# Opening of a linear-attention and expert kernel: other load order, buffers per head pair, and seven PSUM banks for the first products

## The chip, the cores and the metric

The kernel runs on one core of a Trainium2 chip. The metric is the device time of one execution in microseconds (us), median of several executions. Where the time of a profiled execution is meant I say "span": it is some 2 us shorter than the device time. All comparisons use executions in the fast state unless I say otherwise (an execution more than 1.5% above the fastest of the same kernel counts as slow). I call a kernel faster or slower where the 95% interval of the ratio excludes 1. The granted clock is the share of TensorE's full clock that the profile records as granted; 1.00 is full speed. Ratios are the mean time of one kernel's fast runs over that of the other's of the same rounds, so they are not quite the ratio of the medians that I quote.

## The reference, cut to what matters

```python
# q, k, v: (8 batches, 8 heads, 576 rows, 64), fp32
phi = lambda x: where(x > 0, x, exp(x) - 1) + 1
kv  = einsum('bhsd,bhse->bhde', phi(k), v)        # per head: 64 x 64
z   = phi(k).sum(rows)
x   = (phi(q) @ kv) / (phi(q) @ z + 1e-6)         # -> (4608, 512)
p   = domain_probs / domain_probs.sum(-1)
for e in range(4):                                # dense experts
    out += p[:, e] * (relu(x @ w1[e]) @ w2[e])    # 512 -> 1024 -> 512
```

The heads are worked on in four pairs of two (128 partitions each). The experts need x turned (x^T), because the kernel hands the matmuls their operands with the contracted index on the partitions.

## The kernel before: the parts that matter here

Every operation is handed to a planner with a priority, an estimated duration, and keys that it reads and writes. The planner simulates the engines and emits the instructions in the order that this gives. The framework then adds a wait wherever two engines touch the same tile.

The opening handles the first 512 rows of batch 0: four head pairs of attention, whose turned x feeds the first layer (`L681`, later `L761` and near it) and the second layer (`L691`, later `L772`) of the four experts in turn, while the weights arrive. From about 80 us on, the other rows follow in "units" (`L835`, later `L924`). They use the same weights and are bound by TensorE.

PSUM is the memory that TensorE's products are written to. The kernel takes eight tiles of it, of 128 partitions by 512 fp32. I call each of them a bank:

```python
    l1b = [pp.tile([P, 512], FP32, tag=f"l1b{i}", name=f"l1b{i}") for i in range(3)]
    l2b = [pp.tile([P, 512], FP32, tag=f"l2b{i}", name=f"l2b{i}") for i in range(4)]
    at = pp.tile([P, 512], FP32, tag="at", name="at")
    slot = [at[:, i * 2 * DE : (i + 1) * 2 * DE] for i in range(3)]
    tbank = l2b[3].bitcast(FP16)
```

A pair of the opening goes through them so (cut from `attention`, `two=True`, and `turn_x`):

```python
            tq, tk = (l2b[1].bitcast(FP16), "l2b1") if two else (tbank, "l2b3")   # q turned
            # ...
            kvs_, kvk = l2b[2][:, 0 : 2 * DE], ("l2b2k",)                # phi(k)^T v
            # ...
            den = l2b[2][:, 256 : 256 + 2 * C].rearrange("p (c h) -> p c h", h=2)
            # ... numerators go to `at`
            # turn_x: four transposes into tbank (l2b[3]), then a ScalarE copy to xt0
```

The first layer of expert 0 has eight column groups (`fj`) of four products each (`dc`, one for each pair's x^T). A product of 512 columns takes 0.216 us. Four groups have a bank of their own and can take the products of pairs 0 to 2 before pair 3 is ready. The other four run after it:

```python
        banks = [(l1b[i], "l1b%d" % i) for i in range(3)]
        if nb == 4:
            banks += [(l2b[0], "l2b0")]
        # ...
            for dc in range(DC):
                for fj in range(nb):
                    bank, key = banks[(b0 + fj) % nb]
                    p_ = pri + (dc * 4 + fj) * step
                    pl.add("PE", 0.216, p_,
                           lambda fj=fj, bank=bank, dc=dc: mm1(e, fj, bank, (dc,)),
                           r=w1k(e, dc, fj) + (("s4", 1, dc),), w=(key,))
```

In gaps of the opening `keep_warm` issues filler matmuls (`L1075`, later `L1174`), which only keep the array busy.

Of the kernel before, what the change touches and what calls it, by code (L numbers as in the profile page):

```python
# [20 lines left out]
class Plan:  # L21
# [13 lines left out]
    def __init__(self):  # L35
        self.ops = []
        self.wr = {}
        self.rd = {}

    def add(self, eng, dur, pri, fn, r=(), w=(), move=0.0, after=0.0, lead=1.2):  # L40
        n = len(self.ops)
        deps = set()
        for key in r:
            if key in self.wr:
                deps.add(self.wr[key])
            self.rd.setdefault(key, []).append(n)
        for key in w:
            if key in self.wr:
                deps.add(self.wr[key])
            deps.update(x for x in self.rd.get(key, ()) if x != n)  # L50
        for key in w:
            self.wr[key] = n
            self.rd[key] = []
        self.ops.append(
            dict(eng=eng, dur=dur, pri=pri, fn=fn, deps=deps, move=move, after=after, lead=lead, w=w)
        )
        return n

    def deadlines(self):
# [10 lines left out]
        for n, o in enumerate(ops):  # L70
            if o["eng"] != "PE" and o["pri"] >= -99:
# [62 lines left out]
def kernel(  # L134
# [27 lines left out]
    WARM, COLD = 22.0, 28  # L162
    T0, TU = 79.0, 6.4
# [7 lines left out]
    def sb(name, shape, dt):  # L171
# [47 lines left out]
    v00 = vss[1].rearrange("p h c d -> p (h c d)").bitcast(FP16)[:, 2 * C * D :].rearrange(  # L219
        "p (h c d) -> p h c d", h=2, c=C  # L220
    )
    ones = sb("ones", [P, 2, 1], FP16)
    rc4 = sb("rc4", [P, 2 * C], FP32)
# [20 lines left out]
    def lk(i):  # L244

        return ("l2b2k", "l2b2n") if i == 2 else ("l2b%d" % i,)

    def stage_keys(i):

        if i < 2:  # L250
            return ("st", i, 0), ("st", i, 1), ("st", i, 2)
        return ("xp", 0), ("xp", 1), ("u2", 0)
# [35 lines left out]
    def v16(i):  # L288

        flat = vss[i].rearrange("p h c d -> p (h c d)").bitcast(FP16)  # L290
        return flat[:, 0 : 2 * C * D].rearrange("p (h c d) -> p h c d", h=2, c=C)

    def load_pair(b, pr, queue, pri, after=0.0, hold=None):
        hs = slice(2 * pr, 2 * pr + 2)
        n = 3 if b < 2 else 2
        i = rot("stage%d" % n, n) if n == 2 else rot("stage3", 3)
        stage[b, pr] = i
        kk = stage_keys(i)
        vo = vss[i] if b or queue == "SP" else v16(i)
        parts = [(k, kqs[i][:, 0], kk[0]), (v, vo, kk[2]), (q, kqs[i][:, 1], kk[1])]  # L300
        if b == 0:
            parts[1:] = parts[:0:-1]
        for t, o, key in parts:
            if (b, pr, key) == (0, 0, kk[1]):
                load_rest(0, "SP", 0, parts=(0,))
            keys = (key, "v00") if (b, key) == (1, ("st", 1, 2)) else (key,)
            dma(queue, pri, o, t[b, hs, 0:NT].rearrange("h (p c) d -> p h c d", c=C), keys,
                0.7,
                hold="w" if b == 2 else hold if key == kk[0] else None,
                mark="k0" if (b, pr, key) == (0, 0, kk[0]) else None, after=after)  # L310

    def load_rest(b, queue, pri, after=0.0, parts=(0, 1, 2)):
        par = b % 2
        rs = slice(par * R, par * R + R)
        for i in parts:
            t, o = ((k, kqr[rs, 0]), (v, vr[rs]), (q, kqr[rs, 1]))[i]
            dma(queue, pri, o, t[b, :, NT:S].rearrange("h s d -> s h d"), (("str", par, i),),
                1.1,
                hold="w" if b in (2, 3) else None, after=after)
# [26 lines left out]
    def probs(b0, b1, raw, keys, out_key, pri):  # L346
# [7 lines left out]
            r=keys, w=(out_key,))  # L354
# [10 lines left out]
    def rest_maps(b, pe_mode, pri, parts=(0, 1)):  # L365
# [19 lines left out]
        if not pe_mode:  # L385
            pl.add("SP", 1.25, pri + 1, lambda: nc.sync.dma_start_transpose(
                out=qTr[par][:, :, rs], in_=kqpr[rs, 1].rearrange("p h d -> p (h d)")),
                r=("qpr",), w=[("qTr", par, i) for i in range(DC)], move=0.9, lead=0.2)

# [44 lines left out]
    def attention(b, pr, pe_mode, pri, step, two=False):  # L434
# [16 lines left out]
        zi = pr if two else rot("kvz", 2)  # L451
# [8 lines left out]
        if two:  # L460
            vh = v00 if pr == 0 else v16(si)
            vk = "v00" if pr == 0 else sk[2]

        def vcast():
            if two:
                nc.scalar.copy(vh, vs)
            else:
                nc.scalar.copy(vp[:, :, :, 0:D].rearrange("p c h d -> p h c d"), vs)

        order_ = (0, 1)  # L470
        for i in order_:
# [4 lines left out]
            if i == 0 and not (two and pr):  # L476
                pl.add("ACT", 0.52, pri + step, vcast, r=(sk[2],), w=(vk,))
        if pe_mode:

            tq, tk = (l2b[1].bitcast(FP16), "l2b1") if two else (tbank, "l2b3")  # L480

            def turn():
# [4 lines left out]
                if two:  # L487
                    return
# [7 lines left out]
                   r=(("kqp", pi, 1), "ident") + (() if two else ("qpr",)), w=(tk,))  # L496
            pl.add("ACT", 0.5, pri + 3.5 * step, lambda: nc.scalar.copy(  # L497
                qT.rearrange("p c t -> p (c t)"), tq[:, 0:NT]), r=(tk,), w=(("qT", ti),))
            if not two:
                pl.add("DVE", 0.2, pri + 3.5 * step, lambda: nc.vector.tensor_copy(  # L500
                    qTr[par][:, pr, rs], tq[:, NT : NT + R]), r=(tk,), w=(("qTr", par, pr),))
# [6 lines left out]
        if two:  # L508
            kvs_, kvk = l2b[2][:, 0 : 2 * DE], ("l2b2k",)
        kv3 = kvs_.rearrange("p (h e) -> p h e", h=2)  # L510

        def kv():
            for c in range(C):
                if two:
                    nc.tensor.matmul(out=kv3[:, :, 0:D], lhsT=kp[:, c], rhs=vh[:, :, c],
                                     start=(c == 0), stop=False, skip_group_check=True)
                    nc.tensor.matmul(out=kv3[:, :, D:DE], lhsT=kp[:, c], rhs=ones,
                                     start=False, stop=False, skip_group_check=True)
                else:
                    nc.tensor.matmul(  # L520
                        out=kvs_, lhsT=kp[:, c], rhs=vp[:, c], start=(c == 0), stop=False
                    )
# [6 lines left out]
                skip_group_check=two,  # L529
# [7 lines left out]
        pl.add("PE", 0.42 if two else 0.3, pri + 4 * step, kv,  # L537
# [4 lines left out]

        if two:
            den = l2b[2][:, 256 : 256 + 2 * C].rearrange("p (c h) -> p c h", h=2)

            def nd0():
                for c in range(C):
                    nc.tensor.matmul(out=at[:, c * P : (c + 1) * P], lhsT=qT[:, c],
                                     rhs=kvz[:, :, 0:D], start=True, stop=True)
                    nc.tensor.matmul(out=den[:, c], lhsT=qT[:, c],  # L550
                                     rhs=kvz[:, :, D:DE], start=True, stop=True)

            def norm0():
                rc = rc4.rearrange("p (c h) -> p c h", h=2)
                nc.vector.reciprocal(rc, den)
                nc.vector.tensor_tensor(
                    out=xs[:, :, fs].rearrange("p c (h d) -> p c h d", h=2),
                    in0=at.rearrange("p (c h d) -> p c h d", c=C, h=2),
                    in1=rc[:, :, :, None].broadcast_to([P, C, 2, D]),
                    op=AO.mult,  # L560
                )

            pl.add("PE", 0.36, pri + 5 * step, nd0, r=(("qT", ti), ("kvz", zi)),
                   w=("at", "l2b2n"))
            pl.add("DVE", 0.83, pri + 5.5 * step, norm0, r=("at", "l2b2n"),
                   w=[("x", par, pr, c) for c in range(C)])
            return
# [77 lines left out]
    def sums_w2(e, pri):  # L645
# [11 lines left out]
        for o, a, b_, r, w in (  # L657
# [5 lines left out]
            pl.add("DVE", 0.62, pri, two(o, a, b_), r=r, w=w)  # L663


    def turn_x(pr, pri):
        fs = slice(pr * P, (pr + 1) * P)

        def go():
            for c in range(C):  # L670
                nc.tensor.transpose(
                    out=tbank[:, c * P : (c + 1) * P], in_=x_b[0][:, c, fs], identity=identh
                )

        pl.add("PE", 0.25, pri, go, r=[("x", 0, pr, c) for c in range(C)] + ["ident"], w=("l2b3",))
        pl.add("ACT", 0.5, pri + 0.5, lambda: nc.scalar.copy(xt0[:, pr, :], tbank[:, 0:NT]),
               r=("l2b3",), w=(("s4", 1, pr),))

    def mm1(e, fj, bank, dcs):
        for dc in dcs:  # L680
            nc.tensor.matmul(  # L681
                out=bank,
                lhsT=w1_sb[e][:, dc, fj * P : (fj + 1) * P],
                rhs=xt0[:, dc, :],
                start=(dc == 0),
                stop=(dc == DC - 1),
# [18 lines left out]
    def first_l1(e, pri, step, nb):  # L705
        ht = []
        banks = [(l1b[i], "l1b%d" % i) for i in range(3)]
        if nb == 4:
            banks += [(l2b[0], "l2b0")]
        ht = [rot("ht", len(hts)) for _ in range(FC)]  # L710

        def relu(fj, bank, key, pr_):
            pl.add("ACT", 0.5, pr_, lambda: nc.scalar.activation(hts[ht[fj]], bank, AF.Relu),
# [3 lines left out]
        if nb:  # L717
            b0 = cnt.get("l1", 0) if nb < 4 else 0
            for dc in range(DC):
                for fj in range(nb):  # L720
                    bank, key = banks[(b0 + fj) % nb]
                    p_ = pri + (dc * 4 + fj) * step
                    pl.add("PE", 0.216, p_,
                           lambda fj=fj, bank=bank, dc=dc: mm1(e, fj, bank, (dc,)),
                           r=w1k(e, dc, fj) + (("s4", 1, dc),), w=(key,))
                    if dc == DC - 1:
                        relu(fj, bank, key, p_ + 0.2)
            done = nb
            if nb == 4:
# [282 lines left out]
    load_pair(0, 0, "SP", 0)  # L1012
    load_rest(0, "SP", 0, parts=(1,))
    load_pair(0, 1, "POOL", 0, hold="k0")
    load_pair(0, 2, "POOL", 0)
    rest_maps(0, True, 3, (0,))
    for pr in range(DC):
        if pr == 3:
            load_pair(0, 3, "POOL", 0)
            load_w1(0, range(DC))  # L1020
            probs(0, 2, p5_b, ("p5",), "pnat0", 24)
            load_w2(0)
            load_rest(0, "POOL", 0, parts=(2,))
        attention(0, pr, True, 2.5 + pr, 0.4, two=True)
# [113 lines left out]
```

## Time and profile before

| | before |
|---|---|
| device time, median of 3 | 498.4 us (498.26 to 498.58) |
| span of the profiled execution | 496.6 us |
| TensorE busy | 485.1 us, 98% |
| x^T of the last pair complete | 22.35 + 0.59 = 22.94 us |
| first layer of expert 0 done | 27.56 + 0.16 = 27.72 us |
| first product of the units | 80.60 us |

How to read it: TensorE is busy nearly all the time, so only an earlier start of its useful work, or fewer fillers, can shorten the kernel. I take the end of the first layer as 0.16 us after the start of the second layer's first matmul, because consecutive matmuls overlap in the records (they start 0.216 us apart and are recorded as 0.38 us long). The prediction below shows the lines. The start of the units is the second checkpoint:

```profile
80.60 0.61 PE L835 MATMUL l1b<-xT,w 128*128 128x128 f16 x8
```

(TensorE timeline of the kernel before: start, length, engine, line, operation, output<-inputs, shapes, count.) From here to the end of the span it is 416.0 us. From the first second-layer matmul (27.56) to here it is 53.04 us, in which TensorE doesn't wait.

### The profile page before, as it was taken

The page shows a single profiled execution, that of the slowest core. Times are in us where ns is not written, and L with a number is a line of the kernel's source. Part 1 is how long each engine was busy: PE and PEld are TensorE (multiplying, and loading weights), DVE is VectorE, ACT ScalarE, POOL GpSimd, SP SyncE. Part 2 cuts the span into 40 slices and gives each one's busy share as a digit, 9 for nine tenths or more (in the row PEclk, how much of TensorE's full clock was granted, in tenths as well). Part 3 has the DMA queues.
Part 4 walks back from the last instruction along what each step waited for, and adds up shares of the span by engine and source line. Part 5 has one row for each costly group of instructions (what it writes and reads, how often), then busy time and mean ns, then how long its engine had stood idle before and what let it go on. Part 6 is the DMA issues. An engine that isn't in the chain of part 4 may idle for free.

```text
span 496.6 us, 15010 instructions
## 1 busy us (share of the span) xinstructions
PE 485.1 (98%) x6109; PEld 430.4 (87%) x6109; DVE 408.6 (82%) x1033; ACT 366.8 (74%) x690; POOL 41.8 (8%) x67
## 2 busy tenths in 40 slices
PE   6899999999999999999999999999999999999995
PEld 5544547999999999999999999999999999999995
DVE  5778998988998999899988899889988676767664
ACT  5636758978977798769876988689766767676641
POOL 7655700000000000000000000000000000000000
PEclk9999999999999999999999999999999999999998
DMA  8999979856784774765855766755623333523211
GB/s 231 203 233 211 264 148 215 196 117 165 121 170 118 172 173 121 130 170 124 161 136 158 141 150 127 174 132 119 161 54 86 42 90 44 77 55 86 45 44 42
DMA packets 125573, 67.11 MB, mean 135 GB/s; under 512 B 95520, under 2 KB 119600, under 8 KB 125504
## 3 DMA queue, kind: packets, MB, share of 16 engines
q1 hardware_dynamic: 116112, 51.79, 47.8%
q0 software_dynamic: 9232, 14.10, 13.9%
q8 instruction: 47, 0.77, 0.7%
q10 hardware_dynamic: 160, 0.26, 0.2%
q14 instruction: 22, 0.18, 0.1%
HBM read 45.16 MB, written 9.44 MB: 110 GB/s over the span
## 4 chain that ended last, share of the span: by engine, by line
PE 94%; ACT 2%; DMA 1%; DVE 1%; issue 1%; SPq 0%; DVEq 0%
PE l1b L835 40%; PE l2b L911 38%; PE l2b L691 6%; PE l1b L681 5%; PE at L571 2%; PE at L520 1%; DMA vs<-in_v_dram 1%; PE l2b L1075 1%; ACT xp L795 1%; SPq L262 0%; DVE ot L975 0%; ACT h L849 0%; ACT qT L497 0%; PE at L523 0%; ACT ek L472 0%
## 5 line engine op out<-in xcount | busy, mean ns | idle before, releaser
L835 PEld LDWEIGHTS <-w 128*128 128x128 f16 x2048 | 133.4, 98 | 5.1
L849 ACT ACTIVATE h<-l1b 128x512 f16<-128x512 f32 x128 | 76.8, 600 | 53.6 <-PE l1b L835 48.4
L911 PE MATMUL l2b<-w,h 128*128 128x256 f16 x768 | 114.9, 273 | 0.0
L911 PE MATMUL l2b<-t,s 128*128 128x256 f16 x768 | 114.4, 273 | 0.0
L835 PEld LDWEIGHTS <-w1x 128*128 128x128 f16 x1536 | 100.1, 98 | 3.9 <-issue 0.2
L911 PEld LDWEIGHTS <-s 128*128 128x128 f16 x1024 | 90.9, 98 | 6.6
L855 DVE CUSTOM_DVE_ANT_0 h<-l1b,p 128x512 f16<-128x512 f32 x64 | 44.1, 689 | 46.2 <-PE l1b L835 42.8
L795 ACT ACTIVATE xp<-x,p_nat 128x512 f16<-128x512 f16 x112 | 77.6, 721 | 0.9 <-DVE x L584 0.5
L835 PE MATMUL l1b<-xT,w 128*128 128x128 f16 x1024 | 78.1, 219 | 0.0
L835 PE MATMUL l1b<-xs,w 128*128 128x128 f16 x1024 | 78.0, 219 | 0.0
L835 PE MATMUL l1b<-xs,w1x 128*128 128x128 f16 x1024 | 77.9, 219 | 0.1
L911 PEld LDWEIGHTS <-h 128*128 128x128 f16 x768 | 67.4, 98 | 4.5
L897 DVE TENSOR_TENSOR s<-h 128x512 f16<-128x512 f16 x128 | 53.8, 420 | 2.1
L852 ACT COPY l1b<-l1b 128x512 f32<-128x512 f32 x64 | 36.7, 574 | 12.6 <-PE l1b L835 11.9
L852 ACT COPY u<-l1b 128x512 f32<-128x512 f32 x64 | 37.5, 586 | 11.1 <-PE l1b L835 10.8
L855 DVE CUSTOM_DVE_ANT_0 h<-l1b,u 128x512 f16<-128x512 f32 x64 | 43.8, 684 | 1.1 <-PE l1b L835 0.4
L852 ACT COPY p<-l1b 128x512 f32<-128x512 f32 x64 | 37.4, 584 | 8.9 <-PE l1b L835 7.2
L472 ACT ACTIVATE ek<-kq 128x512 f16<-128x512 f32 x60 | 37.9, 632 | 3.4 <-DMA kq<-in_k_dram 2.3
L813 DVE TENSOR_TENSOR xs<-xT,xs 128x256 f16<-128x256 f16 x128 | 36.8, 287 | 3.4
L835 PE MATMUL l1b<-xT,w1x 128*128 128x128 f16 x512 | 39.0, 219 | 0.0
L911 PE MATMUL l2b<-w,s 128*128 128x256 f16 x256 | 38.4, 273 | 0.0
L457 DVE TENSOR_TENSOR kqp<-ek,kqp 128x512 f16<-128x512 f16 x64 | 27.2, 425 | 5.9 <-ACT ek L472 1.6
(128 smaller groups left out, 576.8 us busy)
## 6 DMA issues: line engine op xcount, KB each, us to landing
w<-in_moe_w_dram POOLq DMA_DIRECT2D x32, 256.0 KB, 8.2
out_dram<-ot SPq DMA_DIRECT2D x16, 512.0 KB, 3.2
kq<-in_k_dram SPq DMA_DIRECT2D x25, 256.0 KB, 3.4
kq<-in_q_dram SPq DMA_DIRECT2D x25, 256.0 KB, 3.6
vs<-in_v_dram SPq DMA_DIRECT2D x25, 256.0 KB, 3.7
kq<-in_k_dram POOLq DMA_DIRECT2D x5, 256.0 KB, 7.1
kq<-in_q_dram POOLq DMA_DIRECT2D x5, 256.0 KB, 6.1
xT<-xp SPq DMA_TRANSPOSE x64, 3.1
```

Source lines behind the costliest of these rows:

```text
L457: nc.vector.tensor_tensor(out=o, in0=ek[:, i], in1=o, op=AO.min)
L472: pl.add("ACT", 0.55, pri + i * step, lambda i=i: nc.scalar.activation(ek[:, i], kq[:, i], AF.Exp), r=(sk[i],), w=(("ek", ei, i),))
L681: nc.tensor.matmul(out=bank, lhsT=w1_sb[e][:, dc, fj * P : (fj + 1) * P], rhs=xt0[:, dc, :], start=(dc == 0), stop=(dc == DC - 1),)
L691: nc.tensor.matmul(out=bank, lhsT=hts[ht[fj]][:, c * P : (c + 1) * P], rhs=w2_sb[e][:, fj, :], start=(fj == 0), stop=(fj == FC - 1),)
L795: pl.add("ACT", 0.6, pri, lambda c=c, src=src, ps=ps: nc.scalar.activation(xp[:, c, :], src, AF.Copy, scale=ps), r=r, w=(("xp", xi, c),))
L813: lambda o=o, a=a, b_=b_: tt(out=o, in0=a, in1=b_, op=AO.subtract),
L835: nc.tensor.matmul(out=bank[:, fc * P : (fc + 1) * P], lhsT=wt[:, kc, fc * P : (fc + 1) * P], rhs=r[:, kc, :], start=(start and fc == 0 an ...
L849: return lambda: nc.scalar.activation(o, bank, AF.Relu)
L852: return lambda: nc.scalar.copy(o, bank)
L855: return lambda: nc.vector._custom_dve(TENSOR_ADD_SAT, out=o, in0=bank, in1=t, s0=BIG, s1=0.0)
L897: pl.add("DVE", 0.36, U(n + 1) + d - 0.5, lambda i=i, a=a, b_=b_, alu=alu: tt(out=s4[:, i], in0=a, in1=b_, op=alu), r=r, w=(Q(i),))
L911: nc.tensor.matmul(out=l2b[bank][:, half * HD : (half + 1) * HD], lhsT=a[:, c, :], rhs=w[:, c], start=(opens and first and c == 0), stop=( ...
```

## The change

The intent is to let the pairs run through the opening without waiting for each other's buffers and for TensorE to have more first-layer products that it can run early. The diff, cut to its core:

```diff
+    v_o = [ ... ]                       # v of the four pairs, each its own place
+    kqp_o = kqp_b + [ ... ]             # phi(k), phi(q) per pair, in room of later weight sums
+    ek_o = ek_b + [ ... ]
+    def first_attention(pr, pri, step):
+        ni = pr % 2
+        num = (at, l2b[1])[ni]                                   # numerators: two banks
+        tq = tbank[:, ni * NT : (ni + 1) * NT]                   # q turned: l2b[3]
+        kv3 = l2b[2][:, 0 : 2 * DE].rearrange("p (h e) -> p h e", h=2)
+        d0 = 136 + ni * 2 * C
+        den = l2b[2][:, d0 : d0 + 2 * C].rearrange("p (c h) -> p c h", h=2)
+        xt = l2b[2].bitcast(FP16)[:, NT : 2 * NT]                # x turned: l2b[2] too
+        ...
+        parts = 2 if pr == DC - 1 else 1                         # last pair in two halves
```
```diff
-        if nb == 4:
-            banks += [(l2b[0], "l2b0")]
+        if nb > 3:
+            banks[2:] = [(l2b[0], "l2b0"), (at, "at"), (l2b[3], "l2b3"), (l2b[1], "l2b1")]
+            banks += [(l1b[2], "l1b2")]
...
+            if nb > 3 and fj in RELU:            # RELU = (0, 2, 4, 6): half the relus on VectorE
+                pl.add("DVE", 0.62, pr_, lambda: nc.vector.tensor_scalar(
+                    hts[ht[fj]], bank, 0.0, None, AO.max), r=(key,), w=(HTK[ht[fj]],))
...
-    load_pair(0, 0, "SP", 0)
-    load_rest(0, "SP", 0, parts=(1,))
-    load_pair(0, 1, "POOL", 0, hold="k0")
-    load_pair(0, 2, "POOL", 0)
+    load_first("SP", -9, k, 0, mark="k0")
+    load_first("SP", -8, q, 0)
+    load_first("SP", -7, k, 1)
+    for g in range(DC):
+        load_first_rest(k, k_r, "ACT" if g < 2 else "SP", -6, "k_r", g)
+    for g in range(DC):
+        load_first_rest(v, v_r32, "SP", -4, "v_r32", g)
+    load_first("SP", -3, q, 1)
+    load_first("POOL", 0, v, 0, hold="k0")
...                                              # k2 q2 v1, a quarter of w1, k3 q3 v2 v3
-    ht = first_l1(0, 17.5, 0.1, 4)
+    ht = first_l1(0, 17.5, 0.1, 7)
...
-        nc.tensor.matmul(out=l2b[1][:, 256:512], lhsT=identh,      # filler
+        nc.tensor.matmul(out=l1b[2][:, 256:512], lhsT=identh,
```

## The prediction

> **What bounds the kernel now.** I read the share of busy time first, then the TensorE timeline in order of time, then who waits for whom on TensorE, and last the DMA issues with their landings. The page says that TensorE is the bound:
>
> ```profile
> PE 485.1 (98%) x6109; PEld 430.4 (87%) x6109; DVE 408.6 (82%) x1033; ACT 366.8 (74%) x690; POOL 41.8 (8%) x67
> PE 94%; ACT 2%; DMA 1%; DVE 1%; issue 1%; SPq 0%; DVEq 0%
> ```
>
> The change touches only the opening, so what counts is when TensorE becomes dense with useful work. The TensorE timeline shows it (start, length, line, out<-in, count; L1075 is filler that only keeps the array busy, L671 turns x, L681 is the first product of expert layers, L691 the second):
>
> ```profile
> 21.93 0.39 PE L671 MATMUL l2b<-s,x 128*128 128x128 f16 x4
> 22.15 1.04 PE L1075 MATMUL l2b<-qTr,s 128*128 128x256 f16 x8
> 23.02 0.81 PE L681 MATMUL l1b<-s,w 128*128 128x512 f16 x3
> 23.89 0.38 PE L1075 MATMUL l2b<-qTr,s 128*128 128x256 f16 x2
> 24.11 3.62 PE L681 MATMUL l1b<-s,w 128*128 128x512 f16 x16
> 27.56 5.34 PE L691 MATMUL l2b<-w,h 128*128 128x512 f16 x24
> 32.74 1.89 PE L681 MATMUL l1b<-s,w 128*128 128x512 f16 x8
> ...
> 49.75 0.22 PE L571 MATMUL at<-kvz,qT 128*128 128x130 f16 x1
> 49.81 0.22 PE L571 MATMUL at<-kvz,qTr 128*128 128x130 f16 x1
> 49.87 4.48 PE L681 MATMUL l1b<-s,w 128*128 128x512 f16 x20
> ```
>
> The last filler ends at 24.3. From there the waits view has no TensorE wait at all, to the end of the kernel: every microsecond by which the dense part starts earlier is worth a microsecond, unless a new wait appears. In the ScalarE timeline the last piece of x^T is copied out at 22.35 + 0.59 = 22.94:
>
> ```profile
> 22.35 0.59 ACT L676 COPY s<-l2b 128x512 f16<-128x512 f16 x1 [1.48 <-PE l2b L671]
> ```
>
> So 27.72 - 22.94 = 4.8 us pass between the last x^T and the end of the first product (16 matmuls of 0.216 us on fj 4 to 7 alone are 3.45), because only four PSUM banks were filled beforehand.
>
> The second resource is the DMA. Two rows by stretch (last columns: granted clock, DMA share, GB/s) and the issue that matters most later (the last quarter of expert 2's first weights; last number: us from issue to landing):
>
> ```profile
> 20.00:22.50 2.50, 2.50 (x27) 1.65 (x26) 1.49 (x6) 0.88 (x3) 1.46 (x3) 1.00 1.24 204
> 45.00:50.00 5.00, 5.00 (x35) 2.70 (x34) 4.08 (x9) 2.41 (x6) 3.37 (x6) 1.00 1.12 249
> 39.60 0.53 POOL L262 DMA_DIRECT2D w<-in_moe_w_dram x1 [1.15 <-DMA vs<-in_v_dram]
> w<-in_moe_w_dram POOLq DMA_DIRECT2D x1, 256.0 KB, 8.1
> ```
>
> The DMA share is above 1.0 in every stretch from 5 to 65 us, and the issues wait for earlier landings: the DMA is full for the whole first eighth of the kernel. It is not on the end's path only because each weight lands a little before its use. Issue plus time to landing, against first use: w1 of expert 1, last quarter, 22.10 + 8.9 = 31.0, needed at 27.72 + 6.9 (the 32 matmuls of L691) = 34.6 if the order were plain: slack 3.6. **w1 of expert 2: 39.60 + 8.1 = 47.7, used at 49.87: slack 2.2.** w1 of expert 3: 56.6 + 7.1 = 63.7, used at 65.64: slack 1.9. All second weights have 3 us or more.
>
> **What the Trainium skill says.** "DMA: Bandwidth & Descriptors", section "Issuing engines are not separate DMA queues": transfers of all queues run on the same 16 engines and interleave; another issuer saves only issue time. The trace agrees: with one software queue active after 8 us the share is already 1.1 to 1.2. So spreading the loads over queues buys no bandwidth here. The same page, "Why small descriptors are slow", puts a fixed cost on each packet; in this trace's packet records 1024 packets of 256 B (the k and v rest rows) took 19.4 ns each, 1.24 us over 16 engines, while 1 KB packets took 69 ns (median 46): slower per byte, but only slightly. "TensorE: Matmul & The Clock Gate", Part 1: about 3.4 us of idleness halves the clock. The trace shows a granted clock of 1.00 in every stretch, with filler in the gaps, so it shows no such fall. "VectorE: DVE Perf Modes", "Why PSUM operands drop a tier": fp32 from PSUM runs at 1x. The trace agrees: L748, a one-source operation from PSUM, takes 0.74 us alone, against 0.60 us for ScalarE's relu (L713).
>
> **The change, part by part.**
>
> *Loads.* Kept: all k, q, v bytes. Rest rows of k and v: 1024 packets of 256 B become 512 of 512 B; between the medians 18 and 46 ns I estimate 27 ns, so 0.9 us in place of 1.24. v of pair 0 goes from fp32 (256 x 69 ns / 16 = 1.1 us) to the converting queue (256 x 64 ns / 16 = 1.0). Together the DMA work in front of all later weights shrinks by about 0.4 us. Order: from the first software packet (6.7 us) I add v0 1.0, k2 and q2 1.4, v1 1.0, w1 quarter 1.4, k3 and q3 1.4, v2 and v3 2.0, and 0.7 for q1 beside them: 15.6 minus little, against the measured 14.56 for v3 before. The inserted w1 quarter accounts for it. The three other quarters at 1.35 each then land at about 19.5 (before: 12.3 + 7.5 = 19.8). So the last operand of the first product comes hardly earlier.
>
> *Chain of the pairs.* Own buffers per pair and separate banks for scores, turns and x^T remove the serialisation by shared buffers. Pair 3 becomes load-bound: v3 at 15.5, its product 0.5, copy 0.45, then in halves numerator 0.2, norm 0.5, turn 0.2, copy 0.35, second half 0.4 later, with five hops of some 0.1: x^T complete at 18.5 to 19 instead of 22.94. ScalarE has room: 4 pairs x (2 x 0.63 + 0.59 + 0.42 + 0.59) = 11.4 us plus 0.7 for the rests, from 3.7 on, gives 16 at the least. The gate is then w1's last quarter, 19.6.
>
> *Seven banks.* After that gate there remain 7 banks x 0.216 = 1.5 and one fj of 0.87, plus 0.3 for its bank's relu on VectorE (0.74) : 22.3 instead of 27.72. Four relus move to VectorE, 4 x 0.74 = 3.0 us, into a stretch where it idles (28.9 to 32.1 now). **Opening alone: 5.4 us earlier.**
>
> *What the DMA leaves of it.* Allow for the 0.4 us by which weights come earlier, for the three matmuls (0.65 us) that can run before the last quarter is needed, and take 0.2 for landing to matmul. Room at expert 1: 3.6 + 0.4 + 0.65 - 0.2 = 4.5. At expert 2: 2.2 + 0.85 = 3.0. At expert 3: 1.9 + 0.85 = 2.8, but the change moves its last two quarters in front of pair 3 of batch 1, three loads of 0.7, so 4.9. The least is **3.0, at expert 2**. TensorE would reach the first product of expert 1 and of expert 2 too early and wait there about 1 to 2 us each; 2.4 of the 5.4 us go back. From 50 us on everything is about 3 us earlier, and the rest is TensorE-bound. I take off 0.2 for joints in a newly planned order: 498.4 - 2.8 = **495.6 us**.
>
> **Rivals.**
> 1. *The whole opening gain arrives* (5.4 us: 493.0). For: the software queue's issues also wait for buffers that an earlier TensorE would free. Against: most of its waits are put down to weight landings, and the DMA share leaves nothing to speed up.
> 2. *Little or nothing arrives* (497.5 to 498.5). The small loads of the sync queue cost about 0.5 to 0.6 us of issue each, as now, so its ten issues last to 7 us; if q1 or the rests are late, the stream slips, w1 with it, and the slack at expert 2 shrinks one for one. Also VectorE is busy 4.6 to 4.9 of each 5 us from 50 to 70: less time before the units' first operands may turn into a TensorE wait at about 78.
> 3. *A clock loss.* The filler ends at the first use of the seventh bank (near 12 us). If gaps after it last long enough, matmuls run at half speed for some us: 1 to 3 us lost, 497 to 499. Against: 21 + attention matmuls, some 8 us, fall into 12 to 20 us, so the array is nearly full.
>
> **Range and chances.** The expert-2 room holds 3.0 with about 1 us of doubt from the DMA stream either way; rival 1 reaches 493 only if the stream speeds up, rivals 2 and 3 end near 498. Range 494.0 to 497.8. Two per cent is 10 us, more than the whole opening gain: within 2% 0.98, faster 0.01, slower 0.01.
>
> **What would show it.** Right: x^T complete near 19, the first product of expert 0 done near 22.3, w1 of expert 2 landing near 47.3 and a TensorE wait for that DMA just before expert 2's first product at about 47, the next wait before expert 1's at 30 to 31; the unit line L835's successor starting about 3 us before 80.6. Wrong: no DMA wait on TensorE at 25 to 50 with a gain of 5; a last x^T after 21; waits for VectorE at 70 to 80; a granted clock under 0.95 in a stretch of the opening; or a DMA stream shifted by more than 1 us.

## The result, and the profile after

The changed kernel took 497.98 us (median of 3; 497.66 to 499.0) against 498.4. The ratio is 0.9996, with a 95% interval from 0.9973 to 1.0019. A second comparison in five rounds (below) gave 497.96 us against 498.67, ratio 0.999. So the change is within 2%, as predicted, but the predicted gain of 2.8 us is not there: 497.98 lies 0.18 us above the range.

| | before | after | predicted |
|---|---|---|---|
| span | 496.6 | 495.8 | |
| pair 0's copy of x^T starts | 14.88 | 13.82 | |
| x^T complete | 22.94 | 22.68 + 0.37 = 23.05 | 18.5 to 19 |
| first layer of expert 0 done | 27.72 | 26.60 + 0.16 = 26.76 | 22.3 |
| first product of the units | 80.60 | 79.66 | about 77.6 |

From the page of the changed kernel, the busy times and the chain that ended last:

```profile
PE 485.8 (98%) x6108; PEld 430.3 (87%) x6108; DVE 411.5 (83%) x1041; ACT 365.2 (74%) x687; POOL 41.1 (8%) x66
...
PE 97%; DVE 1%; ACT 1%; issue 0%; DVEq 0%
```

TensorE is as busy as it was and is still the bound; VectorE has 3 us more. The units start 0.94 us earlier. From there to the end it is 495.8 - 79.66 = 416.1 us and from the first second-layer matmul to there 79.66 - 26.60 = 53.06 us, both as before:

```profile
79.66 0.61 PE L924 MATMUL l1b<-xT,w 128*128 128x128 f16 x8
```

So all of the gain and all of the shortfall are made before the second layer of expert 0 starts. The ScalarE timeline of the changed kernel has the copies of x^T (`L571`; the last pair comes in two halves; the square bracket is the idle time before and what ended it):

```profile
13.82 0.59 ACT L571 COPY s<-l2b 128x512 f16<-128x512 f16 x1
...
16.45 0.59 ACT L571 COPY s<-l2b 128x512 f16<-128x512 f16 x1
...
19.86 0.59 ACT L571 COPY s<-l2b 128x512 f16<-128x512 f16 x1 [0.50 <-PE l2b L517]
21.95 0.37 ACT L571 COPY s<-l2b 128x256 f16<-128x256 f16 x1 [1.50 <-PE l2b L532]
22.68 0.37 ACT L571 COPY s<-l2b 128x256 f16<-128x256 f16 x1 [0.36 <-PE l2b L532]
```

The last x^T is no earlier than before. Pair 0 is ahead (13.82; before 14.88), but 3.4 us pass between the copies of pairs 1 and 2, and from the start of pair 0's copy to the complete x^T it is 23.05 - 13.82 = 9.23 us. I call this the *pairs' time*. In the kernel before it was 22.94 - 14.88 = 8.06 us: the change made it 1.17 us longer. It turned out to be the best yardstick: where pair 0 starts varies by some 0.7 us among the runs with this order, and what follows repeats within some 0.06 us.

Pair 0's lead need not come from the loads. The filler of the kernel before writes to `l2b1`, the bank of the turned q, and waits three times for a copy out of it, 2.6 us in all. The longest of these waits held TensorE until 14.02, although pair 0's x was ready to be turned at 13.62 (VectorE's last step on it, 12.93 + 0.69; the lines are from the TensorE and the ScalarE timeline of the kernel before):

```profile
14.02 0.60 PE L1075 MATMUL l2b<-qTr,s 128*128 128x256 f16 x4 [1.22 <-ACT qT L497]
14.88 0.59 ACT L676 COPY s<-l2b 128x512 f16<-128x512 f16 x1 [0.38 <-PE l2b L671]
```

A run below that keeps the old loads, moves the filler and adds two banks starts pair 0's copy at 13.81. The TensorE timeline of the changed kernel shows what it waits for (`L517` computes denominators, `L532` turns x):

```profile
17.08 0.16 PE L517 MATMUL l2b<-s,qT 128*128 128x2 f16 x1 [0.39 <-ACT s L571]
...
20.50 0.17 PE L517 MATMUL l2b<-s,qT 128*128 128x2 f16 x1 [0.60 <-ACT s L571]
...
22.37 0.27 PE L532 MATMUL l2b<-s,x 128*128 128x128 f16 x2
22.48 0.38 PE L761 MATMUL l2b<-s,w 128*128 128x512 f16 x1
...
25.52 1.25 PE L761 MATMUL l1b<-s,w 128*128 128x256 f16 x6
26.60 1.67 PE L772 MATMUL l2b<-w,h 128*128 128x512 f16 x7
```

The denominators don't need the turned x of the pair before. They wait for its copy (`L571`) because both lie in bank `l2b2`. VectorE's reciprocals of the denominators (`L522`) wait in the same way:

```profile
18.29 0.21 DVE L522 RECIPROCAL rc<-l2b 128x8 f32<-128x8 f32 x1 [0.93 <-PE l2b L506]
...
20.86 0.18 DVE L522 RECIPROCAL rc<-l2b 128x4 f32<-128x4 f32 x1 [1.63 <-PE l2b L517]
```

The denominators of pair 2 were written by 17.5 (the last `L517` of that pair starts at 17.33), but the reciprocal starts only at 18.29, after the k-v product (`L506`) of the *next* pair, because that is in `l2b2` as well. The kernel before had the k-v product and the denominators in this bank, and x^T in another. The change gave x^T to the crowded one. The Trainium skill, "PSUM — Partial Sum Buffer", section "PSUM bank collisions raise a hardware error", says that two engines must not access one bank in the same partitions at the same time, reads included, and that software has to guard by the bank rather than by the address. The emitted waits agree: one pair's reciprocal waits 0.93 us for the other pair's product at other columns of the bank. The waits are put in by the framework, tile by tile; no run here shows what the chip would do without them.

Second, the banks. The last turn starts at 22.37; from 22.48 to 26.60 first-layer products run without a gap. That is 4.1 us, or 19 products of 0.216 us, where the kernel before had 20. Of the 21 products that seven banks could take for pairs 0 to 2, only 13 had run by then. `at`, `l2b1` and `l2b3` hold numerators and turned q of the pairs until late: the first product into `at` starts at 20.61. The x^T of pair 2, at 20.45, is late as well.

The loads did as predicted or better. The POOL timeline and the DMA issues (the last number: us from issue to landing) for the last quarter of expert 2's first weights:

```profile
37.98 0.53 POOL L292 DMA_DIRECT2D w<-in_moe_w_dram  x1 [0.64 <-DMA vs<-in_v_dram]
```
```profile
w<-in_moe_w_dram POOLq DMA_DIRECT2D x1, 256.0 KB, 7.9
```

It landed at 37.98 + 7.9 = 45.9 and was first used at 48.79: no wait. In TensorE's timeline there is no wait from 22.4 to the start of the units, and the granted clock was 1.00 in every stretch of the opening. The 0.94 us that did arrive are fillers (about 1.1 us between the last turn of x and the first layer before) that useful products replaced, plus one product fewer, less the later last turn.

One more difference does not cost time here but matters below. The windows by stretch (busy us of PE, PEld, DVE, ACT, POOL, then granted clock, DMA share, GB/s), before and then after:

```profile
25.00:30.00 5.00, 5.00 (x25) 2.29 (x24) 3.55 (x7) 3.18 (x7) 3.21 (x5) 1.00 1.13 208
30.00:35.00 5.00, 5.00 (x27) 2.16 (x26) 2.89 (x5) 0.93 (x2) 2.80 (x4) 1.00 1.22 229
```
```profile
25.00:30.00 5.00, 5.00 (x29) 2.60 (x27) 4.72 (x13) 2.19 (x4) 3.16 (x5) 1.00 1.13 203
30.00:35.00 5.00, 5.00 (x24) 2.23 (x23) 4.96 (x9) 0.43 (x1) 2.88 (x5) 1.00 1.22 242
```

VectorE, with 1.5 to 2 us of room in each before, is now full.

### The profile page after: what moved, and what is told of

Read it like the earlier page. It is cut to its first block, busy times and chain, and to the rows that moved or that the text cites. A ratio compares the mean times of both kernels' runs of the same rounds, so it can differ in the third digit from the quotient of the medians.

```text
span 495.8 us, 15025 instructions
## 1 busy us (share of the span) xinstructions
PE 485.8 (98%) x6108; PEld 430.3 (87%) x6108; DVE 411.5 (83%) x1041; ACT 365.2 (74%) x687; POOL 41.1 (8%) x66
## 4 chain that ended last, share of the span: by engine, by line
PE 97%; DVE 1%; ACT 1%; issue 0%; DVEq 0%
PE l1b L924 40%; PE l2b L1000 39%; PE l2b L772 6%; PE l1b L761 5%; PE at L664 2%; PE l1b L1174 2%; PE at L640 1%; PE l2b L506 0%; DVE ot L1064 0%; PE l2b L761 0%; ACT s L571 0%; PE at L643 0%; PE l2b L532 0%; DVE x L523 0%; PE l2b L616 0%
## 5 line engine op out<-in xcount | busy, mean ns | idle before, releaser
L605 ACT ACTIVATE ek<-kq 128x512 f16<-128x512 f32 x54 | 33.7, 628 | 0.1
L986 DVE TENSOR_TENSOR s<-s,h 128x512 f16<-128x512 f16 x64 | 27.2, 424 | 5.6
```

What stands on the lines that cost most here:

```text
L605: pl.add("ACT", 0.55, pri + i * step, lambda i=i: nc.scalar.activation(ek[:, i], kq[:, i], AF.Exp), r=(sk[i],), w=(("ek", ei, i),))
L986: pl.add("DVE", 0.36, U(n + 1) + d - 0.5, lambda i=i, a=a, b_=b_, alu=alu: tt(out=s4[:, i], in0=a, in1=b_, op=alu), r=r, w=(Q(i),))
```

## The experiments

My theory after the comparison: (a) the shared bank `l2b2` serialises the pairs; (b) banks that pairs hold until late take few products early. The rivals: the loads or the other shared buffers set the last x^T; the DMA stream or VectorE would swallow an earlier opening anyway.

To move x^T to a bank of its own, that bank has to be taken from the first layer's seven. So the control is the changed kernel with six.

### Control: six banks

```diff
-    ht = first_l1(0, 17.5, 0.1, 7)
+    ht = first_l1(0, 17.5, 0.1, 6)
-        nc.tensor.matmul(out=l1b[2][:, 256:512], lhsT=identh,      # filler
+        nc.tensor.matmul(out=l2b[0][:, 256:512], lhsT=identh,
```

> Control for the next two runs: the changed kernel with six first banks instead of seven and the filler writing to another bank. My theory (one PSUM bank holds the k-v product, the denominators and x^T of every pair, so three engines take turns on it) expects the changed kernel's picture: x^T complete near 23.1 us, L1 of expert 0 done at 26.8 to 27.1, TensorE waits of about 1.0 us for the x^T copy, time within 0.5 us of the changed kernel. The rivals expect the same.

Measured: 498.55 us against 498.81, ratio 0.9997 (0.9984 to 1.0009). x^T complete 23.24 + 0.37 = 23.61, first layer done 27.54, units from 80.44. The first and the last copy of x^T, from ScalarE's timeline:

```profile
14.38 0.58 ACT L571 COPY s<-l2b 128x512 f16<-128x512 f16 x1
...
23.24 0.37 ACT L571 COPY s<-l2b 128x256 f16<-128x256 f16 x1 [0.36 <-PE l2b L532]
```

TensorE's waits (line waited for: total, times, longest):

```profile
PE l2b L517 <- ACT s L571: 1.0, 2, 0.6
PE at L515 <- ACT kvz L511: 1.0, 1, 1.0
PE l2b L532 <- DVE x L523: 0.7, 2, 0.4
```

The pairs' time is 23.61 - 14.38 = 9.23 us, exactly that of the changed kernel, so the control is sound. That x^T is 0.56 us later stems from the start of pair 0, before which TensorE waited 1.0 us for a k-v copy (at 11.37). The first layer and the units are 0.78 us later; the other 0.22 us go with the bank that is missing. (I had expected the first layer done at 26.8 to 27.1.)

### x^T in a bank of its own: two tries

```diff
-        xt = l2b[2].bitcast(FP16)[:, NT : 2 * NT]
+        xt = l1b[2].bitcast(FP16)[:, NT : 2 * NT]
+    A["l1b2"] = ["l2b2x"]                      # planner: l1b2 and x^T are one resource
```

> Same instruction order on TensorE up to the last turn of x, but x^T has a bank of its own. My theory: the TensorE wait for the x^T copy (1.0 us, twice) and VectorE's wait of 0.7 us for it go away; x^T of pair 3 complete 1 to 2 us earlier (21.0 to 22.2), L1 of expert 0 done about 1 us earlier than in the control, and the time with it, about 0.8 to 1.5 us less. Rival (the chain is set by the loads or by ScalarE's and VectorE's own work): x^T within 0.3 us of the control.

Measured: 558.36 us, ratio 1.1193. This was my mistake. The planner's key for bank `l2b2` still listed x^T, so from then on the plan tied a first-layer bank to a second-layer bank for the whole kernel. The total says nothing about the theory. The opening, emitted before the tie could act, does: TensorE's order was that of the control until then, and the pairs' time was 21.89 - 14.34 = 7.55 us.

The mended version also takes x^T out of the key:

```diff
-        return ("l2b2k", ("l2b2n", 0), ("l2b2n", 1), "l2b2x") if i == 2 else ("l2b%d" % i,)
+        return ("l2b2k", ("l2b2n", 0), ("l2b2n", 1)) if i == 2 else ("l2b%d" % i,)
```

> The same as six_xt_own, whose added planning key tied the second product's banks to the first product's through the whole kernel and so spoilt the order after the opening; here every engine's instruction order equals six_banks, only the bank of x^T differs. In six_xt_own the opening itself showed x^T complete at 21.9 against 23.6 in six_banks. My theory: this 1.7 us arrives at the end in full, so the time is 1.5 to 1.8 us below six_banks. Rival (DMA room): part of it is lost in a new TensorE wait between 25 and 50 us.

Measured: 496.89 us (496.14 to 497.42) against 499.05, ratio 0.9956 (0.9941 to 0.9972). A listing of the two kernels' instructions showed every engine's order to be identical to that of the control; only the bank of x^T differs. ScalarE's first and last copies:

```profile
13.65 0.58 ACT L572 COPY s<-l1b 128x512 f16<-128x512 f16 x1
...
20.10 0.37 ACT L572 COPY s<-l1b 128x256 f16<-128x256 f16 x1 [0.82 <-PE l1b L533]
20.83 0.37 ACT L572 COPY s<-l1b 128x256 f16<-128x256 f16 x1 [0.36 <-PE l1b L533]
```

Pair 0's copy starts at 13.65, so the pairs' time is 21.20 - 13.65 = 7.55 us, as in the first try and 1.68 less than the control's 9.23. From pair 0's copy to the second layer it is 24.96 - 13.65 = 11.31 us, 1.69 less than the control's 27.38 - 14.38 = 13.00. (The times themselves differ by 2.4 us, because pair 0 happened to start 0.73 earlier.) The waits of `L517` for the copy of x^T are gone. One bank assignment, with nothing else changed, is worth 1.7 us in the opening: part (a) is shown for x^T. But from the second layer to the units it is now 79.49 - 24.96 = 54.53 us instead of 53.06: 1.5 us are given back. A new wait has appeared, at 49.49:

```profile
49.49 0.22 PE L665 MATMUL at<-kvz,qT 128*128 128x130 f16 x1 [0.91 <-DVE x L678]
```

(TensorE timeline.) That is attention of batch 1 waiting for VectorE. It explains 0.9 of the 1.5 us.

### A bank each for k-v product, denominators and x^T

```diff
-        num = (at, l2b[1])[ni]
+        num = at
-        den = l2b[2][:, d0 : d0 + 2 * C].rearrange("p (c h) -> p c h", h=2)
+        den = l2b[1][:, d0 : d0 + 2 * C].rearrange("p (c h) -> p c h", h=2)
         xt = l1b[2].bitcast(FP16)[:, NT : 2 * NT]
-            banks[2:] = [(l2b[0], "l2b0"), (at, "at"), (l2b[3], "l2b3"), (l2b[1], "l2b1")]
+            banks[2:] = [(l2b[0], "l2b0"), (l2b[3], "l2b3"), (l2b[2], "l2b2k"), (at, "at"), (l2b[1], "l2b1")]
```

The first try had the same mistake in the planner's key:

> The k-v product, the denominators and x^T each in a bank of its own (the numerators of all pairs share one). My theory: also the waits of ScalarE's and TensorE's k-v steps for the reciprocal go; x^T complete 1.5 to 3 us before the control (20.0 to 21.5) and L1 of expert 0 done 1.5 to 2.5 us before it; if DMA does not bind, the time falls by as much. Rival of the loads: nothing beyond 0.3 us. Rival of my prediction's DMA room: the gain at L1 arrives only up to about 4 us at the end, so it should arrive here in full.

Measured: 568.13 us, again for the planner's sake. Its pairs' time was 20.82 - 13.80 = 7.02 us. The mended one:

> As six_all_own with the key mended and the order of six_banks. The opening of six_all_own had L1 of expert 0 done at 24.7 us against 27.5 in six_banks. My theory: about 2.6 to 2.9 us below six_banks at the end, near 495.8, faster than both kernels; no TensorE wait on DMA, as the room at expert 2 is 3 us or more. If the room of my prediction is right and no more, it is just used up.

Measured: 496.84 us (496.19 to 497.05) against 499.05, ratio 0.9955 (0.9942 to 0.9968). It is faster than before, and, measured in other rounds, also below the changed kernel's 497.98. Against the control's 498.55, also of other rounds, it is 1.7 us, not the 2.6 to 2.9 that I expected. x^T is complete at 20.51 + 0.37 = 20.88, so the pairs' time is 20.88 - 13.92 = 6.96 us, 2.27 less than the control's. From pair 0's copy to the second layer it is 24.64 - 13.92 = 10.72 us, 2.28 less. The units start at 78.34, that is 53.70 us after the second layer: 0.64 us are given back. TensorE's waits up to the units, without the filler's at the very start:

```profile
PE l2b L509 <- DMA t<-in_v_dram: 0.5, 1, 0.5
PE at L518 <- ACT kvz L514: 0.3, 1, 0.3
PE at L518 <- ACT qT L565: 0.3, 1, 0.3
PE at L667 <- DVE x L680: 0.2, 1, 0.2
```

Now only one load and the first pairs' short hops are left in the opening. This run also shows the limit of the whole idea. From its first first-layer product at 15.25 to the end of that layer at 24.80, TensorE has practically no gap (the windows show 2.00, 2.00 and 1.97 busy of each 2 us from 16 to 22). These 9.55 us are 32 products, 6.9 us, and 2.6 us of pairs' work. With these banks freed, TensorE itself is what takes the time.

### Fewer banks

```diff
-            banks[2:] = [(l2b[0], "l2b0"), (at, "at"), (l2b[3], "l2b3"), (l2b[1], "l2b1")]
-            banks += [(l1b[2], "l1b2")]
+            banks[3:] = [(l2b[0], "l2b0"), (at, "at"), (l2b[3], "l2b3"), (l2b[1], "l2b1")]
-    ht = first_l1(0, 17.5, 0.1, 7)
+    ht = first_l1(0, 17.5, 0.1, 4)
```

> The changed kernel with four first banks as before the change, all four free early. If the further banks are what brings the 0.9 us of the changed kernel: L1 of expert 0 done about 0.6 to 1.0 us later than in the changed kernel (27.3 to 27.8) and the time back at the kernel before. If only the four early banks get filled before the last x^T anyway and the others add nothing: within 0.3 us of the changed kernel.

Measured: 500.55 us against 498.81, ratio 1.0033 (1.002 to 1.0047). The profiled execution, however, took 1301.2 us and can't be compared.

> The changed kernel with four first banks, all of them free early, once more for a profile in the ordinary state (its first profile fell on an execution of 1301 us). Theory (of the seven banks three are held by the pairs until late, so only some products are lost by leaving them out): fillers come back, the turn of x is complete near 23.0 to 23.6 as with six and seven, 28 whole-matmul equivalents or so are left after it, first layer of expert 0 done at 28.0 to 29.0, unit start 1.0 to 2.0 later than the changed kernel's 79.66. Rival (banks don't matter, the turn of x alone does): first layer done at 26.8 to 27.5 as with seven and six.

Measured: 500.08 us (one run, so its state is unknown). The pairs' time is 23.26 - 14.02 = 9.24 us: the banks of the first layer don't touch it. From pair 0's copy to the second layer it is 27.84 - 14.02 = 13.82 us, against 12.78 (26.60 - 13.82) with seven and 13.00 with six. So banks five to seven are worth 1.04 us, and of that 0.45 is a wait for VectorE's relu at 24.4 that only the kernel with four has. My count of three products for each bank gives 9 x 0.216 = 1.94 us. With four banks the second layer starts at 27.84, *later* than before the change (27.56): the load order, the buffers per pair and the halves, taken together with the crowded bank, bring nothing at that point. As that bank costs 1.7 us in the control, they may win something that it takes back; no run has four banks without it.

### Six first banks in the kernel before

```diff
-        if nb == 4:
-            banks += [(l2b[0], "l2b0")]
+        if nb > 3:
+            banks += [(l2b[0], "l2b0"), (l2b[1], "l2b1"), (at, "at")]
-    ht = first_l1(0, 17.5, 0.1, 4)
+    ht = first_l1(0, 17.5, 0.1, 6)
```

(The filler moves to `l1b[2]`, out of the bank of the turned q. So two things change.)

> One part of the change alone on the kernel before: six first banks (two of them free only late), filler in another bank, loads and attention chain as before. If the further banks make the changed kernel's gain: L1 of expert 0 done about 1 us earlier (26.5 to 27.0) and the time 0.7 to 1.2 us below before. If the gain needs the new load order and chain: within 0.3 us of before.

Measured: 502.26 us against 499.05, ratio 1.0069 (1.0051 to 1.0086): slower, and outside both forecasts. Yet its second layer starts at 25.16, which is 2.4 us earlier than before and 1.4 us earlier than in the changed kernel. Pair 0's copy starts 1.07 us earlier (13.81; the filler's waits for the turned q are gone), and from there to the second layer it is 11.35 us in place of 27.56 - 14.88 = 12.68. So these two small parts alone bring more at this point than the whole change. The gain is lost later, in a newly planned order with waits that the kernel before has not:

```profile
PE l1b L835 <- DVE h L855: 1.5, 1, 1.5
PE l2b L396 <- DVE kqpr L375: 1.0, 1, 1.0
PE l1b L681 <- DMA w<-in_moe_w_dram: 0.7, 1, 0.7
PE at L571 <- DVE x L584: 0.7, 1, 0.7
```

The units start at 81.55, 56.4 us after the second layer in place of 53.04. The early opening was worth nothing here, because what follows it, VectorE above all by these waits, did not keep up. How much of this is the order and how much VectorE's load I can't tell from this run.

### Would the DMA have taken the gain back?

The prediction's room of 3 us in the DMA stream was never reached. To reach it I took 24 matmuls of expert 0 (5.2 us) out of the best kernel so far. Its output is wrong, which doesn't matter for the time.

```diff
         for dc in dcs:
+            if e == 0 and dc in (1, 2):
+                continue
...
         for fj in fjs:
+            if e == 0 and fj > 5:
+                continue
```

> Wrong result on purpose. six_all_own2 with 24 matmuls of 0.216 us left out of expert 0's two products (5.2 us of TensorE work, all in the opening), no other change of order. Theory of the DMA room: TensorE reaches expert 1 before its first weights (landing near 30.4 us) and expert 2 before its own (near 46 us), waits for DMA there about 1 to 3 us, and the time falls by only 2 to 4 us against six_all_own2. Rival (no room limit, earlier buffers speed the loads up): about 5 us less, no DMA wait on TensorE.

Measured: 496.73 us, ratio 0.9954 (0.9938 to 0.997): the same as without the cut. The second layer of expert 0 ends 3.7 us earlier (27.87 instead of 31.55), and the units start at 78.65, not even earlier than 78.34. TensorE's timeline:

```profile
28.72 0.39 PE L766 MATMUL l1b<-s,w 128*128 128x512 f16 x1 [0.26 <-DMA w<-in_moe_w_dram]
29.94 1.25 PE L766 MATMUL l1b<-s,w 128*128 128x512 f16 x5 [0.83 <-DMA w<-in_moe_w_dram]
32.74 0.37 PE L441 MATMUL l2b<-s,kqpr 64*128 64x64 f16 x4 [1.55 <-DVE ot L844]
33.04 1.89 PE L766 MATMUL l1b<-s,w 128*128 128x512 f16 x4
```

First comes the DMA: 1.1 us for the weights of expert 1. Then comes VectorE, 1.55 us, which is busy all the time (1.99 and 2.00 us of 2 from 30 to 34). And then the matmuls run slower: four take 1.89 us, against 1.03 us for four in the full-speed stretches. The windows show a lower granted clock (columns as above, after PEld: DVE, ACT, POOL, then the clock):

```profile
32.00:34.00 2.00, 1.26 (x7) 0.62 (x7) 2.00 (x5) 0.00 (x0) 0.83 (x2) 0.67 1.21 251
34.00:36.00 2.00, 2.00 (x9) 0.90 (x8) 1.97 (x6) 0.60 (x1) 1.12 (x2) 0.50 1.09 352
```

So the room behind the opening is real and limited, as the prediction argued for the DMA at expert 1. But two more limits lie right beside it: VectorE and the clock. This run can't say how large each would be alone.

### A seventh bank in the new assignment

```diff
-    ht = first_l1(0, 17.5, 0.1, 6)
+    ht = first_l1(0, 17.5, 0.1, 7)
```

> The kernel with a bank of its own for the k-v products, the denominators and the turns of x, with seven first banks in place of six; the seventh is the bank of the denominators. Theory (a bank beyond six is held by the pairs until some 21 us, so it can take at most one or two products before the last turn of x): turn of x complete 20.8 as with six, first layer of expert 0 done at 24.4 to 24.8 instead of 24.80, unit start within 0.3 of 78.34, time ratio 0.995 to 0.997. Rival (each bank takes three products of 0.216 us out of the tail, as my prediction counted): first layer done at 24.15, unit start 77.7, ratio 0.994.

Measured: 498.86 us (497.17 to 499.51) against 498.67, ratio 1.0002 (0.999 to 1.0014). From pair 0's copy to the second layer it is 24.86 - 14.12 = 10.74 us, against 10.72 with six: the seventh bank brings nothing. That refutes the count of three products for each bank. It fits part (b), since the bank holds denominators until the end of the pairs, but doesn't test it: TensorE had no gap there with six either, so another bank could not have helped. The time missed what either theory expected: the units start at 79.07, 54.2 us after the second layer, and 417.4 us follow. The waits show new ones, in the first batches' attention and in the units:

```profile
PE at L518 <- ACT kvz L514: 1.0, 1, 1.0
PE l1b L927 <- ACT l1b L944: 0.6, 2, 0.3
PE at L643 <- ACT vp L605: 0.6, 1, 0.6
```

TensorE's order differs from that with six in many places up to 360 us, so I can't name a single cause. Its median is 2.0 us above that with six (496.84, in other rounds); how much of this the new order makes isn't shown.

### Is VectorE what takes the rest back?

```diff
-    LATE, RELU = 0.5, (0, 2, 4, 6)
+    LATE, RELU = 0.5, ()
```

> The same kernel with six first banks, with all eight relus of expert 0's first layer on ScalarE instead of half of them on VectorE; the order of TensorE is the same. It asks whether VectorE is what takes back 0.64 us of the 2.74 us between the first layer and the start of the units. Theory (VectorE is nearly full from 25 to 50, and the 0.2 us wait on it at 48 is the tip of that): 4 relus of 0.68 us leave VectorE, that wait goes and the units start 0.2 to 0.6 earlier than 78.34, unless ScalarE's eight relus in a row make the second layer wait some 0.5 us at 25. Rival (it isn't VectorE): unit start within 0.1 of 78.34 or later, ratio 0.9955 or above.

Measured: 496.12 us (495.89 to 496.39) against 498.67, ratio 0.9952 (0.994 to 0.9964), span 493.9. TensorE's order is identical to that of the kernel with six banks and a bank each. The second layer starts at 24.73, as late as there (24.64), and the units at 77.79, 0.55 us earlier. That is 53.06 us after the second layer, the figure of a kernel without waits. So the whole gain of the opening arrives: 27.56 - 24.73 = 2.83 us at the second layer, 80.60 - 77.79 = 2.81 at the units, 496.6 - 493.9 = 2.7 in the span. All of TensorE's waits after the opening are gone:

```profile
PE l2b L1177 <- DVE qTr L1101: 2.6, 1, 2.6
PE at L518 <- ACT kvz L514: 0.8, 1, 0.8
PE l2b L509 <- DMA t<-in_v_dram: 0.8, 1, 0.8
PE at L518 <- ACT qT L565: 0.2, 1, 0.2
```

(The 2.6 us is the filler's wait at the very start, which the other kernels have too.) VectorE was busy 2.83 of 5 us from 25 to 30, where it had 4.79 with the relus. As TensorE's order is the same in both traces, they can be laid side by side: the 0.64 us fall at two places, 0.27 at 34.7, where TensorE starts just after VectorE's copy of a turned q has ended, and 0.38 at 48.3, the wait for VectorE in the list of waits. So VectorE was what took the gain back between 25 and 50, shown in the traces by moving four relus and nothing on TensorE. The total times can't show it: the ratios of the two kernels, from different rounds, are 0.9955 and 0.9952. This is the best version I found: it beats the kernel before by 2.5 us of medians in the same rounds, and the changed kernel by 1.8, as the next run of the same rounds shows.

### The changed kernel once more

> The changed kernel, unchanged, timed in five rounds beside the kernel before, because its first comparison had three rounds, its interval reached from 0.9973 to 1.0019 and its opening gain in the traces was only 0.94 us (first product of the units 80.60 to 79.66). Theory (the gain is filler replaced by a few useful products, 0.9 us, and all of it stays): ratio 0.998, between 0.997 and 0.999. Rival (the gain is given back by waits in the units, or my prediction of 2.8 us was true and three rounds were too few): 1.000, or 0.9945.

Measured, in the same rounds as the last two: 497.96 us (497.68 to 498.38) against 498.67, ratio 0.999 (0.9977 to 1.0003). The 0.7 us agree with the 0.94 us at the units, though the interval still includes no difference. The second layer started at 26.87 this time, 0.27 later than in the first profile, but the pairs' time was 23.32 - 14.09 = 9.23 us and pair 0's copy to the second layer 12.78 us, both exactly as there. What varies is when pair 0 starts.

## Why the prediction was right or wrong

- **Within 2%**: right; it rested on the size of the whole opening.
- **Where the gain can come from**: right. From the start of the units on, both kernels take 416 us, and only the time to dense useful work counts.
- *Loads*: right for expert 0. The last quarter of its first weights was issued at 11.95 and took 7.2 us, so it landed at 19.15 (predicted about 19.5). Expert 2's landed at 45.9, 1.4 us before the predicted 47.3; a stream shifted by more than 1 us was one of the prediction's own signs of being wrong. Why it ran ahead was not examined.
- *Chain of the pairs*: **this step failed first.** It said "Own buffers per pair and separate banks for scores, turns and x^T remove the serialisation by shared buffers". The banks aren't separate: the diff places the k-v product, the denominators and x^T of all pairs in `l2b[2]`, and I took the buffers in SBUF for the whole of it and did not look up the bank of each PSUM tile. x^T was complete at 23.05, not at 18.5 to 19, and the pairs' time grew from 8.06 to 9.23 us. Giving x^T its own bank, in the same instruction order, brings it from 9.23 to 7.55 us; a bank for each of the three, to 6.96. Even then x^T is complete only at 20.88. "Pair 3 becomes load-bound" did not come true either: in that run its v landed at 15.3 (predicted 15.5), but its k-v product started at 16.58, and from there to x^T it took 4.3 us, where the prediction's terms add up to 3.1. What held these two was not examined.
- *Seven banks*: **this step failed too**, in "After that gate there remain 7 banks x 0.216 = 1.5 and one fj of 0.87". It took 21 products as done before the gate. It was 7 at 20.6 and 13 when the last turn of x began, at 22.37. Three of the seven banks held the pairs' data until late, and x^T of pair 2 was complete only at 20.45; the runs don't separate these two. So 19 products' worth of time remained instead of 11. Three more banks were worth 1.04 us; with the pairs' banks apart, the seventh was worth nothing.
- **What was never added up**: even with the pairs' banks apart, the first layer ends at 24.80 and not at 22.3. TensorE has 9.55 us of work from 15.25 on. My 22.3 leaves 7.05 us for it. Moving some of that work ahead could help little: from 12 to 16 us this kernel's TensorE had 0.75 us idle and 0.87 us of filler, so I estimate 24.80 - 1.6 = 23.2 as the earliest end. Of the 4.46 us between 22.3 and the measured 26.76, some 2 are thus the banks (12.78 - 10.72 = 2.06 from pair 0's copy to the second layer) and the other 2.4, as I read it, the missing sum of TensorE's own work.
- *What the DMA leaves of it*: not tested by the change, because so little arrived. With expert 2's weights at 45.9, the room there was about 4.4 us by the prediction's own sum, not 3.0 (an estimate: 3.0 + 1.4). With the opening made shorter by force, TensorE did wait 1.1 us for expert 1's weights, at 28.5 to 29.9; the wait predicted at expert 2 was not seen in any run. The 2.83 us of the best version fit in either room without a wait. The step left out VectorE between 25 and 50 us, which took 0.64 us of the gain in the kernel with a bank each and made TensorE wait 1.5 us in the shortened one.
- **Rivals**: the time fell into that of rival 2 (497.5 to 498.5), but not for its reasons. The loads did not slip, and VectorE did not hold up the changed kernel. The clock loss of rival 3 was not seen in the changed kernel; it was seen in the shortened one.

The size 2.8 us was by chance near what a repaired change gives (2.2 us of medians with a bank each, 2.5 us with the relus moved as well). That doesn't make its steps right.

## What to carry to other kernels

Write down for each PSUM tile of a chain the bank, not the columns, and who touches it, fillers included: here one bank shared by three stages made three engines take turns, even across pairs that don't depend on each other. Count a buffer as additional only from the moment when its former user lets go of it. And before believing an earlier gate, add up the work that the bounding engine still has to do between the last load and the target, and the room of the next engine after it.

## What the Trainium skill lacked or had wrong

- "PSUM — Partial Sum Buffer" has the rule on collisions, but nothing on what keeping it costs in time. Here, moving one tile out of a shared bank, in an unchanged order of instructions, took 1.68 us off a chain of 9.23. The page's summary tells to read from another bank, or at least from other partitions, than a running matmul writes; what it costs when stages of one chain take turns on a bank, no page says.
- "TensorE: Matmul & The Clock Gate", Part 1, puts the fall to half speed down to an idle window of about 3.4 us. It also tells of a kernel in which frequent short gaps made the clock go up and down, but not how long the gaps were or how busy TensorE was. In the shortened kernel the longest single wait was 1.55 us, with waits of 0.26 and 0.83 us before it and TensorE busy 2.1 of the 4 us from 28 to 32; the granted clock then was 0.67 and 0.50 in the two stretches from 32 to 36. In the kernel before with six banks, waits of 1.03 and 0.38 us between 28 and 30 left it at 1.00.
- No page tells of a whole execution like this: one execution of the kernel with four banks took 1301.2 us, with 536 ns for a matmul of 256 columns instead of 273 and a recorded granted clock of 1.00. Its other runs took 500.26 to 500.87. I don't know the cause.
